# Linear attention and channel mix on one core: q of batch 3 by TensorE, g moved into the x product, and new numbers in the planner

## The chip, the core and the metric

One core of a Trainium2 chip runs the whole kernel. The metric is device microseconds of one execution, the median of several. Times and ratios are of fast runs, except where a slow one is named. A program on one core has no second die to compare with, so "fast" here means within 1.5% of the fastest run of the same kernel. The span of a profile is about 2 us shorter than the time of the same execution (237.8 against 239.78 us before), so spans are compared with spans and times with times.

## The reference, cut to what matters

```python
# 8 batches, 8 heads, 576 positions, head dim 64; d_model 512, d_ff 1024
kv  = einsum('bhsd,bhse->bhde', k, v)
u   = einsum('bhsd,bhde->bhse', q, kv)
x   = u / sqrt(mean(u*u, -1) + 1e-6) * g_norm       # then heads side by side: (8, 576, 512)
x_prev = x shifted by one position
xk, xr = mu_k*x + (1-mu_k)*x_prev, mu_r*x + (1-mu_r)*x_prev
out = sigmoid(xr @ w_r) * (relu(xk @ w_k)**2 @ w_v)
```

The attention of a batch ends in xk and xr. The mix works on nine groups of 512 positions; group g needs the batches that its positions lie in (group 1 needs batches 0 and 1).

## The kernel before

The kernel is written as small pieces of work. A planner inside it (a greedy list scheduler in Python) walks through the pieces with estimated lengths, picks an engine for each, and so fixes the order of the instructions of every engine. The chip then runs each engine's list in that order. A wrong estimate costs nothing by itself, but an instruction that the plan puts too early holds up everything behind it on its engine.

```python
class Planner:
    SHUN = {"DVE": 0.5}          # a penalty when VectorE is one of the choices
    ...
    def run(self, warm=None):
        ...
            ways.append((t + us + self.SHUN.get(eng, 0.0), t, eng))   # earliest end wins
        ...                                                           # (cut)
            if p.land:                                # a piece that starts a DMA
                came = p.end + 1.2
                if p.eng == "POOL":
                    dma = max(dma, came) + p.land
                    p.end = dma + 0.8                 # when the data is believed there
                else:
                    p.end = max(came + p.land, min(dma, came + 2 * p.land)) + 0.8
                    dma = max(dma, came) + p.land
```

Loads of k, v and q are issued by GpSimd (POOL in the profile), one after the other; each has two buffers, so the load of batch b+2 waits until batch b's buffer has been read. q has to be transposed. Batches 0 to 2 do it on TensorE, six 96x128 blocks for each of four head pairs, with a copy out of PSUM (the memory that TensorE writes its products to). Batches 3 to 7 do it by one DMA transpose on the SP queue:

```python
if b >= 3:
    def q_dma(_):
        nc.sync.dma_start_transpose(out=get(qT)..., in_=qin.t...)
    m = add(f"qT dma {b}", {"SP": 3.2}, q_dma, bufs=[qin, qT], due=due(30),
            deps=[loaded[("q", b, 0)]], land=2.5)
else:
    ...                                               # 24 transposes, 4 copies
```

The norm is spread back over 64 columns per head by a product with a matrix selg (0 or g), and x is u times the result, read from PSUM:

```python
nc.vector.tensor_tensor(out=selg[:, tl], in0=rows..., in1=g_all..., op=ALU.mult)     # x4
...
nc.vector.tensor_mul(out=xT.t[:, hs, xs], in0=get(uT)[...], in1=ps.t[:, 0:step, 0:HS])
```

When the plan leaves TensorE idle before the first mix product, it fills the gap with products of zeros ("fillers", one per 0.23 us of the planned gap), which are meant to keep TensorE's clock up. Until 80 us of the plan it also fills some later gaps, before a product that opens a new buffer in PSUM.

Of the kernel before, what the change touches and what calls it, by code (L numbers as in the profile page):

```python
# [36 lines left out]
class Planner:  # L37
    LAT = {"PE": 0.25, "ACT": 0.15, "DVE": 0.12, "POOL": 0.15, "SP": 0.0}

    SWITCH = {"PE": 0.11, "ACT": 1.28}  # L40
    SHUN = {"DVE": 0.5}
    SLACK = {"PE": 0.0}
    STAY = {"PE": 4.0, "ACT": 4.0}

# [33 lines left out]
    def run(self, warm=None):  # L78


        free, order, dma, modes = {}, [], 0.0, {"PE": None, "ACT": None}
        while self.left:
            best = {}
            for p in self.left:
                if any(d.end is None for d in p.deps):
                    continue
                room = self.room(p.bufs)
                if room is None:
                    continue
                ways = []  # L90
                for eng, us in p.on.items():
                    slack = self.SLACK.get(eng, 0.0)
                    t = max(free.get(eng, 0.0), room + slack)
                    for d in p.deps:
                        t = max(t, d.end + (self.LAT[d.eng] + slack if d.eng != eng or d.land else 0.0))
                    ways.append((t + us + self.SHUN.get(eng, 0.0), t, eng))
                _, t, eng = min(ways)
                stay = self.STAY.get(eng, 0.0) if p.mode == modes.get(eng) else 0.0
                best.setdefault(eng, []).append((t, p.due - stay, p))
            picks = []  # L100
            for eng, c in best.items():
                t0 = min(x[0] for x in c)
                picks.append(min((x for x in c if x[0] <= t0 + 0.02), key=lambda x: x[1]) + (eng,))
            t, _, p, p.eng = min(picks, key=lambda x: x[0])
            if warm and p.eng == "PE":
                since, first, until, idle = warm
                gap = t - max(free.get("PE", 0.0), since)
                if first is not None:
                    n, buf = int(gap / 0.23), None
                else:  # L110
                    n, buf = int((gap - 0.3) / 0.23), p.bufs[0] if p.fresh and not p.bufs[0].placed else None
                    n = n if buf is not None and t < until else 0
                if n > 0:
                    order.append(lambda n=n, buf=buf: idle(n, buf))
                if p is first:
                    warm = (since, None, until, idle)
            p.start, p.end = t, t + p.on[p.eng]
            if p.eng in self.SWITCH and p.mode is not None or p.eng == "PE":
                p.end += self.SWITCH[p.eng] * (p.mode != modes[p.eng])
                modes[p.eng] = p.mode  # L120
            free[p.eng] = p.end
            if p.land:

                came = p.end + 1.2
                if p.eng == "POOL":
                    dma = max(dma, came) + p.land
                    p.end = dma + 0.8
                else:
                    p.end = max(came + p.land, min(dma, came + 2 * p.land)) + 0.8
                    dma = max(dma, came) + p.land  # L130
            for b in p.bufs:
                if not b.placed:
                    b.placed = True
                    self.rings[b.tag][self.slots(b.tag)[0][1]] = b
            self.left.remove(p)
            order.append(p)
        for p in order:
            if isinstance(p, Piece):
                p.fn(p.eng)
            else:  # L140
                p()
        return [p for p in order if isinstance(p, Piece)]
# [3 lines left out]
def kernel(  # L146
# [13 lines left out]
    nc = tc.nc  # L160
# [69 lines left out]
    ident8 = const.tile([8, 8], FP32, name="ident8")  # L230
    mu_raw = const.tile([2 * NHP, 128], FP32, name="mu_raw")
    mu_sb = const.tile([128, 2 * NHP], FP32, name="mu_sb")
    g_all = const.tile([128, HD], FP32, name="g_all")
    eps = const.tile([128, 1], FP32, name="eps")
    zeros = const.tile([128, 512], BF16, name="zeros")
    sel = const.tile([128, NHP, 32], BF16, name="sel")
    selg = const.tile([128, NHP, NHP, 2, HD], BF16, name="selg")
    w_r_sb = const.tile([128, NHP, C], BF16, name="w_r")
    w_k_sb = const.tile([128, NHP, F], BF16, name="w_k")
    w_v_sb = const.tile([128, NFC, C], BF16, name="w_v")  # L240
# [4 lines left out]
    def consts_small(_):  # L245
        nc.vector.memset(zeros, 0.0)
        nc.vector.memset(eps, 1e-6)
        ln_table()
        nc.sync.dma_start(out=mu_raw[0:NHP], in_=moe_mu_k.rearrange("(j p) -> j p", p=128))
        nc.sync.dma_start(out=mu_raw[NHP:2 * NHP], in_=moe_mu_r.rearrange("(j p) -> j p", p=128))  # L250
        nc.sync.dma_start(out=g_all, in_=g_norm.rearrange("(o d) -> o d", o=1).broadcast_to([128, HD]))

        nc.vector.memset(sel, 0.0)
        for e in range(2):
            for s in range(NHP):
                nc.vector.memset(sel[64 * e:64 * e + 64, s, 2 * s + e:2 * s + e + 1], 1.0)
# [12 lines left out]
    def consts_selg(_):  # L269

        for tl in range(NHP):
            rows = ident[:, 32 * tl:32 * tl + 2 * NHP].rearrange("p (s e) -> p s e", e=2)
            nc.vector.tensor_tensor(out=selg[:, tl], in0=rows.unsqueeze(3).broadcast_to([128, NHP, 2, HD]),
                                    in1=g_all.unsqueeze(1).unsqueeze(1).broadcast_to([128, NHP, 2, HD]), op=ALU.mult)

    def load_w(dst, src):
        nc.gpsimd.dma_start(out=dst, in_=src.rearrange("(c p) n -> p c n", p=128))
# [8 lines left out]
    def load(b, n, h0, h1, due):  # L286
# [7 lines left out]
        for h in range(h0, h1):  # L294
            loaded[(n, b, h)] = p

    PARTS0 = ((0, 2), (2, 1), (3, 1))
    p_ident = None
    for hp0, n in PARTS0:
# [2 lines left out]
        if p_ident is None:  # L302
            p_ident = add("ident", {"POOL": 0.8}, consts_idents, due=-900 + 0.5)
    p_mu = add("mu", {"DVE": 0.5}, consts_mu, deps=[p_ident], bufs=[p_mu_ps], due=-800)
    p_selg = add("selg", {"DVE": 2.8}, consts_selg, deps=[p_ident], due=-800)
    p_wr = add("load w_r", {"POOL": 0.8}, lambda _: load_w(w_r_sb, moe_w_r), due=-700, land=2.6)
    p_wk = add("load w_k", {"POOL": 0.8}, lambda _: load_w(w_k_sb, moe_w_k), due=-699, land=5.2)
    for n in ("k", "v", "q"):
# [23 lines left out]
    def attention_part(b, part, bufs, ps_buf):  # L332
# [5 lines left out]
        ln, rs = Buf("ln"), Buf("rs")  # L338

        def due(x):  # L340
            return 20 * b - 2 * x if b else -100 - x

        def flat(hp):
            return get(uT)[:, hp].rearrange("q i jj p -> q (i jj p)")
# [14 lines left out]
        def kv_copy(eng, e):  # L359
            for half in range(2):  # L360
# [2 lines left out]

        mm = add(f"kv {b}", {"PE": 0.25 * n}, kv_mm, mode=1, bufs=[pkv, kin, vin, kv], due=due(26),
                 deps=[loaded[(m, b, h)] for m in ("k", "v") for h in (2 * hp0, 2 * (hp0 + n) - 1)] + ([last_rr[0]] if b == 1 else []))
        kvs = [add(f"kv copy {b}", {"DVE": 0.25 + 0.14 * n, "ACT": 0.38 + 0.11 * n}, lambda eng, e=e: kv_copy(eng, e), deps=[mm],
                   bufs=[kv, pkv], due=due(24)) for e in range(2)]


        qts = {}  # L370
        if b >= 3:
            def q_dma(_):
                nc.sync.dma_start_transpose(out=get(qT).rearrange("q h x -> q (h x)").rearrange(
                    "q (y p) -> q y p", p=NP), in_=qin.t.rearrange("p h x -> p (h x)"))

            m = add(f"qT dma {b}", {"SP": 3.2}, q_dma, bufs=[qin, qT], due=due(30), deps=[loaded[("q", b, 0)]], land=2.5)
            qts = {hp: m for hp in hps}
        else:
            for hp in hps:
# [7 lines left out]
                def q_cp(eng, hp, ps):  # L387
                    copy(eng, get(qT)[:, 2 * hp:2 * hp + 2, :], ps.t[:, :, 0:NI * NP])
# [1 line left out]
                ps = ps_buf()  # L390
                m = add(f"qT {b}", {"PE": 0.35}, lambda _, hp=hp, ps=ps: q_tr(_, hp, ps), bufs=[ps, qin, qT], due=due(27),
                        deps=[p_ident, loaded[("q", b, 2 * hp)], loaded[("q", b, 2 * hp + 1)]] + ([last_rr[0]] if b == 1 else []))
                qts[hp] = add(f"qT copy {b}", {"ACT": 0.65, "DVE": 0.75}, lambda eng, hp=hp, ps=ps: q_cp(eng, hp, ps), deps=[m],
                              bufs=[ps, qT], due=due(25))


# [1 line left out]
        for hp in hps:  # L398
# [12 lines left out]
            def u_sq(eng, hp):  # L411
# [3 lines left out]
            ps = ps_buf()  # L415
            m = add(f"u {b}", {"PE": 0.14}, lambda _, hp=hp, ps=ps: u_mm(_, hp, ps), mode=1, deps=kvs + [qts[hp]],
                    bufs=[ps, kv, qT, uT, sq], due=due(22))
            us[hp] = add(f"u copy {b}", {"ACT": 0.69, "DVE": 0.75}, lambda eng, hp=hp, ps=ps: u_cp(eng, hp, ps), deps=[m],
                         bufs=[ps, uT], due=due(21))
            sqs.append(add(f"u sq {b}", {"DVE": 0.46}, lambda eng, hp=hp: u_sq(eng, hp), deps=[us[hp]], bufs=[uT, sq],  # L420
                           due=due(20)))
# [17 lines left out]
            nc.scalar.activation(out=get(rs), in_=ln.t, func=AF.Exp, scale=-0.5)  # L439

        m = add(f"st {b}", {"PE": 0.3}, st_mm, mode=2, deps=sqs, bufs=[pst, sq, ln, rs], due=due(18))
        st = add(f"rs {b}", {"ACT": 0.7}, st_ln, deps=[m], bufs=[pst, ln, rs], due=due(17), mode="ln")


        xms = []
# [1 line left out]
        for hp1 in range(hp0, hp0 + n, step):  # L447
            for half in range(2):
# [11 lines left out]
                def x_mul(_, hp1, cs, xs, ps):  # L460
                    if xT.t is None:
                        nc.vector.memset(get(xT)[:, :, 0:1], 0.0)
                    hs = slice(hp1, hp1 + step)
                    nc.vector.tensor_mul(out=xT.t[:, hs, xs],  # L464
                                         in0=get(uT)[:, hs].rearrange("q h i jj p -> q h (i jj p)")[:, :, cs],
                                         in1=ps.t[:, 0:step, 0:HS])

                ps = ps_buf()
                m = add(f"rr {b}", {"PE": 0.13 * step}, lambda _, hp1=hp1, half=half, ps=ps: rr_mm(_, hp1, half, ps),
# [10 lines left out]
            e.tensor_copy(out=x[:, hsl, 1:NP], in_=x[:, hsl, S:S + NP - 1])  # L480
            e.tensor_tensor(out=get(d)[:, hsl], in0=x[:, hsl, NP:NP + S], in1=x[:, hsl, 0:S], op=ALU.subtract)  # L481

        df = add(f"d {b}", {"DVE": 0.4 * n}, diff, deps=xms, bufs=[xT, d], due=due(11))

        c0 = S * (b % 4)
        order = (("r", xr, NHP), ("k", xk, 0)) if b == 0 else (("k", xk, 0), ("r", xr, NHP))
        for pos, (key, dst, m) in enumerate(order):
# [10 lines left out]
            def blend(_, dst, t):  # L498
# [1 line left out]
                                        op=ALU.add)  # L500

            late = due(10 - 4 * pos) + (50 * pos if b == 0 else 0)
            sc = add(f"t{key} {b}", {"DVE": 0.365 * n, "ACT": 0.7 * n}, lambda eng, m=m, t=t: scale(eng, m, t), deps=[df, p_mu], bufs=[d, t], due=late)
            x_ready[b][key].append(add(f"x{key} {b}", {"DVE": 0.06 + 0.34 * n}, lambda _, dst=dst, t=t: blend(_, dst, t), deps=[sc],
                                       bufs=[xT, t], due=late))

    attention(0, PARTS0)
# [137 lines left out]
```

## Time and profile before

| | before |
|---|---|
| time, median of 3 (lowest to highest); a fourth run came with the result | 239.77 us (239.6 to 240.05) |
| span of the profiled run | 237.8 us |
| TensorE busy | 90% |
| first R product starts | 28.63 us |
| last group (group 8) starts | 214.01 us |

Lines of the page: the span, the busy line, then for TensorE, its granted clock (PEclk, as a share of full speed) and the DMA engines 40 slices of the span (one digit per 5.9 us, in tenths), then the chain of waits by engine and line.

```profile
span 237.8 us, 4055 instructions
...
PE 214.1 (90%) x1669; PEld 103.7 (44%) x1669; DVE 140.7 (59%) x245; ACT 129.5 (54%) x178; POOL 25.1 (11%) x39
...
PE   2989999998583999999898999899899999999981
...
PEclk9999999999887699999999999999999999999997
DMA  3999999999999999999850060024006015015033
...
PE 76%; DMA 8%; DVE 7%; ACT 4%; issue 2%; POOL 1%; DVEq 0%; POOLq 0%
```

PE falls to 5 and 3 tenths in slices 11 and 13 and to no less than 8 anywhere else between head and tail, and PEclk falls to 6 to 8 tenths in slices 11 to 14 (59 to 83 us). The DMA row is at 9 from the second slice to the nineteenth: the loads run without a break until about 110 us. The chain names "DMA qT<-q" for 8% of the span.

In the lines of the mix, L540 is K (xk times w_k), L563 R and L583 V; L354 is kv, L384 a transpose of q, L404 u, L433 the sum of squares, L456 the spreading product, L612 a filler. The stretch from 53.3 to 84.1 us ("the hole" below) in the view of windows (length, then busy time and count of each engine, granted clock, DMA share, GB/s):

```profile
core 0: us, PE busy (x) PEld busy (x) DVE busy (x) ACT busy (x) POOL busy (x), PEclk, DMA share, GB/s
...
53.30:84.10 30.80, 22.45 (x218) 10.10 (x217) 20.89 (x39) 16.34 (x26) 4.62 (x6) 0.83 1.27 195
```

And TensorE's own timeline in it (start and length in us, line, operation, count; in brackets the idle time before it and what ended it):

```profile
57.80 1.89 PE L540 MATMUL mm<-xk,w_k 128*128 128x512 bf16 x8
...
63.25 1.14 PE L354 MATMUL at<-v,k 96*64 96x64 bf16 x48 [2.06 <-DMA v<-in_v_dram]
...
64.77 3.10 PE L540 MATMUL mm<-xk,w_k 128*128 128x512 bf16 x8
...
75.31 0.45 PE L404 MATMUL at<-qT,kv 64*64 64x288 bf16 x4 [4.96 <-DMA qT<-q]
75.69 1.89 PE L540 MATMUL mm<-xk,w_k 128*128 128x512 bf16 x4
...
88.23 1.03 PE L540 MATMUL mm<-xk,w_k 128*128 128x512 bf16 x4
```

Besides 160 small products of attention, this is K and R of group 1; its xk was ready at 57.6 us. They come in parcels between pieces of batches 3 and 4, and each parcel waits for the piece ahead of it: kv of batch 4 for its v (2.06 us), u of batch 3 for the transposed q (4.96 us). After the waits the clock is down: four K products take 1.89 us at 75.69, and 1.03 us at 88.23, when it is up again. TensorE is idle for 8.4 of the 30.8 us (30.80 less 22.45 busy) and runs fillers for 2.8; the rest of what is lost, some 4 us, goes mostly to the slow clock. The wait view (us in total, times, longest) and the SP queue show the transpose and what it blocks:

```profile
POOL q L288 <- DMA qT<-q: 31.9, 2, 16.8
...
PE at L404 <- DMA qT<-q: 5.0, 1, 5.0
...
PE at L354 <- DMA v<-in_v_dram: 2.1, 1, 2.1
```

```profile
55.37 19.71 SPq L373 DMA_TRANSPOSE qT<-q  x2
```

Two transposes are merged in this line, batch 3's among them; it was issued at 55.4 us and landed at 75.3 (19.9 us, the longest by the view of the tile qT). The next load of q may not overwrite the buffer before that, and stands at the head of POOL's list: 16.8 us of the 31.9 us in the first line of the waits.

The head (fillers, the first kv product, the first R product) and the start of the last group.

```profile
4.79 6.21 PE L612 MATMUL mm<-zeros 128*128 128x512 bf16 x18
10.93 0.57 PE L354 MATMUL mm<-v,k 96*64 96x64 bf16 x24
...
28.63 1.89 PE L563 MATMUL mm<-w_r,xr 128*128 128x512 bf16 x8
...
214.01 7.07 PE L540 MATMUL mm<-xk,w_k 128*128 128x512 bf16 x32
```

### The profile page before, as it was taken

The page shows a single profiled execution, that of the slowest core. Times are in us where ns is not written, and L with a number is a line of the kernel's source. Part 1 is how long each engine was busy: PE and PEld are TensorE (multiplying, and loading weights), DVE is VectorE, ACT ScalarE, POOL GpSimd, SP SyncE. Part 2 cuts the span into 40 slices and gives each one's busy share as a digit, 9 for nine tenths or more (in the row PEclk, how much of TensorE's full clock was granted, in tenths as well). Part 3 has the DMA queues.
Part 4 walks back from the last instruction along what each step waited for, and adds up shares of the span by engine and source line. Part 5 has one row for each costly group of instructions (what it writes and reads, how often), then busy time and mean ns, then how long its engine had stood idle before and what let it go on. Part 6 is the DMA issues. An engine that isn't in the chain of part 4 may idle for free.

```text
span 237.8 us, 4055 instructions
## 1 busy us (share of the span) xinstructions
PE 214.1 (90%) x1669; PEld 103.7 (44%) x1669; DVE 140.7 (59%) x245; ACT 129.5 (54%) x178; POOL 25.1 (11%) x39
## 2 busy tenths in 40 slices
PE   2989999998583999999898999899899999999981
PEld 1443454554330355345434466444444444444430
DVE  1436938379487369977973895697487324224222
ACT  2075697828531691994789557666954513604500
POOL 8553021212001320010000000000000000000000
PEclk9999999999887699999999999999999999999997
DMA  3999999999999999999850060024006015015033
GB/s 41 197 207 207 204 207 203 204 204 241 188 160 176 209 202 158 195 256 100 197 123 0 4 176 3 0 61 119 0 0 164 12 26 156 0 28 152 0 88 88
DMA packets 38627, 29.46 MB, mean 124 GB/s; under 512 B 13513, under 2 KB 33489, under 8 KB 38609
## 3 DMA queue, kind: packets, MB, share of 16 engines
q0 software_dynamic: 21008, 16.78, 47.0%
q1 hardware_dynamic: 17600, 12.43, 24.7%
q8 instruction: 13, 0.21, 0.4%
q14 instruction: 6, 0.04, 0.1%
HBM read 33.59 MB, written 9.44 MB: 181 GB/s over the span
## 4 chain that ended last, share of the span: by engine, by line
PE 76%; DMA 8%; DVE 7%; ACT 4%; issue 2%; POOL 1%; DVEq 0%; POOLq 0%
PE mm L540 25%; PE mm L583 24%; PE mm L563 13%; DMA qT<-q 8%; PE mm L612 5%; PE at L404 3%; PE at L456 2%; DVE out L587 2%; DVE xT L464 2%; ACT sig L568 1%; PE at L384 1%; DVE d L481 1%; PE at L433 1%; ACT kv L216 1%; ACT uT L216 1%
## 5 line engine op out<-in xcount | busy, mean ns | idle before, releaser
L540 PE MATMUL mm<-xk,w_k 128*128 128x512 bf16 (+1 forms) x320 | 70.1, 369 | 1.3 <-DVE out L587 1.3
L583 PE MATMUL mm<-w_v,sqk 128*128 128x512 bf16 x288 | 66.2, 379 | 1.9 <-DVE out L587 1.7
L544 ACT ACTIVATE relu<-mm 128x1024 bf16<-128x1024 f32 x36 | 36.8, 1023 | 38.8 <-PE mm L540 37.4
L540 PEld LDWEIGHTS <-w_k 128*128 128x128 bf16 x320 | 30.2, 100 | 31.9 <-issue 5.9
L583 PEld LDWEIGHTS <-sqk 128*128 128x128 bf16 x288 | 27.6, 98 | 32.3 <-issue 2.8
L587 DVE TENSOR_TENSOR out<-mm,sig 128x1024 f32<-128x1024 f32 (+1 forms) x20 | 22.3, 1116 | 27.3 <-PE mm L583 27.2
L547 DVE TENSOR_TENSOR sqk<-relu 128x1024 bf16<-128x1024 bf16 x36 | 24.7, 690 | 19.6 <-ACT relu L544 19.6
L563 PE MATMUL mm<-w_r,xr 128*128 128x512 bf16 x144 | 33.2, 381 | 0.0
L464 DVE TENSOR_TENSOR xT<-uT,at 128x576 bf16<-128x576 bf16 (+1 forms) x31 | 21.8, 732 | 14.0 <-PE at L456 14.0
L496 ACT ACTIVATE t<-d,mu_sb 128x576 bf16<-128x576 bf16 x30 | 21.0, 768 | 16.0 <-DVE d L481 14.6
L216 ACT CAST uT<-at 128x576 bf16<-128x576 f32 x24 | 14.5, 640 | 18.5 <-PE at L404 18.5
L563 PEld LDWEIGHTS <-xr 128*128 128x128 bf16 x144 | 13.7, 98 | 16.7 <-issue 0.7
L568 ACT ACTIVATE sig<-mm 128x1024 bf16<-128x1024 f32 x18 | 18.1, 1023 | 4.3 <-PE mm L563 4.2
L612 PE MATMUL mm<-zeros 128*128 128x512 bf16 x69 | 20.0, 418 | 0.0
L413 DVE TENSOR_TENSOR sq<-uT 128x576 bf16<-128x576 bf16 x32 | 13.9, 455 | 8.1 <-ACT uT L216 7.7
L456 PE MATMUL at<-rs,selg 128*128 128x144 bf16 x120 | 11.8, 229 | 1.8 <-DVE xT L464 1.8
L456 PEld LDWEIGHTS <-selg 128*128 128x128 bf16 x128 | 9.7, 99 | 7.7 <-issue 3.2
L404 PE MATMUL at<-qT,kv 64*64 64x288 bf16 x116 | 8.4, 321 | 5.0 <-DMA qT<-q 5.0
L288 POOL DMA_DIRECT2D q<-in_q_dram x10 | 7.3, 734 | 40.1 <-DMA qT<-q 31.9
L499 DVE TENSOR_TENSOR xk<-t,xT 128x2304 bf16<-128x2304 bf16 (+2 forms) x10 | 11.1, 1114 | 0.5 <-ACT t L496 0.4
L481 DVE TENSOR_TENSOR d<-xT 128x2304 bf16<-128x2304 bf16 (+2 forms) x10 | 11.2, 1118 | 0.3
L288 POOL DMA_DIRECT2D k<-in_k_dram x10 | 7.5, 752 | 35.7 <-PE at L354 32.0
(51 smaller groups left out, 136.7 us busy)
## 6 DMA issues: line engine op xcount, KB each, us to landing
out_dram<-out SPq DMA_DIRECT2D x24, 192.0 KB, 2.5
k<-in_k_dram POOLq DMA_DIRECT2D x7, 576.0 KB, 14.9
v<-in_v_dram POOLq DMA_DIRECT2D x7, 576.0 KB, 18.1
q<-in_q_dram POOLq DMA_DIRECT2D x7, 576.0 KB, 18.0
out_dram<-out SPq DMA_DIRECT2D x24, 128.0 KB, 2.4
out_dram<-out SPq DMA_DIRECT2D x24, 64.0 KB, 2.1
w_k<-in_moe_w_k_dram POOLq DMA_DIRECT2D x1, 1024.0 KB, 11.7
w_v<-in_moe_w_v_dram POOLq DMA_DIRECT2D x1, 1024.0 KB, 22.4
```

The lines of the kernel that those rows point to most:

```text
L216: nc.scalar.copy(out=dst, in_=src)
L456: nc.tensor.matmul(get(ps)[:, i, SEC * c:SEC * c + SEC], selg[:, tl, sub].rearrange("p e d -> p (e d)"), rs.t, start=True, stop=True)
L464: nc.vector.tensor_mul(out=xT.t[:, hs, xs], in0=get(uT)[:, hs].rearrange("q h i jj p -> q h (i jj p)")[:, :, cs], in1=ps.t[:, 0:step, 0:HS])
L496: nc.scalar.mul(out=dst, in_=d.t[:, hp, :], mul=by)
L540: nc.tensor.matmul(get(ps)[:, fc % 2, a0:a1], w_k_sb[:, cc, 128 * fc:128 * fc + 128], xk[:, cc, x0:x0 + a1 - a0], start=(cc == 0), stop=(c ...
L544: nc.scalar.activation(out=get(rt), in_=ps.t, func=AF.Relu)
L547: nc.vector.tensor_mul(out=get(sqk)[:, 2 * f2:2 * f2 + 2, :], in0=rt.t, in1=rt.t)
L563: nc.tensor.matmul(get(ps)[:, ci % 2, :], xr[:, cc, n0:n0 + 128], w_r_sb[:, cc, :], start=(cc == 0), stop=(cc == NHP - 1))
L568: nc.scalar.activation(out=get(sg), in_=ps.t, func=AF.Sigmoid)
L583: nc.tensor.matmul(get(ps)[:, ci % 2, :], sqk.t[:, fc, 128 * ci:128 * ci + 128], w_v_sb[:, fc, :], start=(fc == 0), stop=(fc == NFC - 1))
L587: nc.vector.tensor_mul(out=get(ot)[:, xs, :], in0=ps.t[:, xs, :], in1=sg.t[:, xs, :])
L612: nc.tensor.matmul(get(buf or warm)[:, 0, :], zeros[:, 0:128], zeros, start=True, stop=True)
```

## The change

The intent: keep VectorE's work small (selg becomes a 0/1 matrix that ScalarE copies; g enters the x product as a per-partition scalar), take one more batch of q away from the DMA queues, and tell the planner how long things really take. "due" in the code is the planner's priority: of the pieces that can start equally early on an engine, the one with the smallest due goes first.

```diff
-    SHUN = {"DVE": 0.5}
+    SHUN = {"DVE": 0.1}
...
+                    if eng == "POOL" and p.land and len(queue) >= 8:
+                        t = max(t, queue[-8])
...
-                came = p.end + 1.2
+                came = max(p.end + 1.2, 3.5)
...
-                    p.end = dma + 0.8
+                    p.end = dma + 1.5
+                    queue.append(p.end)
...
-                    p.end = max(came + p.land, min(dma, came + 2 * p.land)) + 0.8
+                    p.end = max(came + p.land, min(dma, came + 2 * p.land)) + 1.5
...
-            nc.vector.tensor_tensor(out=selg[:, tl], in0=rows..., in1=g_all..., op=ALU.mult)
+            nc.scalar.copy(out=selg[:, tl], in_=rows...)
...
-    p_selg = add("selg", {"DVE": 2.8}, consts_selg, ...)
+    p_selg = add("selg", {"ACT": 2.4}, consts_selg, ...)
...
-            return 20 * b - 2 * x if b else -100 - x          # due of attention pieces
+            return 20 * b - 2 * x - 4 if b else -100 - x
...
-        if b >= 3:
+        if b >= DMA_T:                                        # DMA_T = 4
...
-            m = add(f"qT dma {b}", {"SP": 3.2}, ..., land=2.5)
+            m = add(f"qT dma {b}", {"SP": 7.8}, ..., land=3.5)
...
-                    nc.vector.tensor_mul(out=xT..., in0=uT..., in1=ps...)
+                    nc.vector.scalar_tensor_tensor(out=xT..., in0=uT..., scalar=g_col,
+                        in1=ps..., op0=ALU.mult, op1=ALU.mult)
```

Cut: g_col is loaded by two small DMAs in place of the broadcast g_all; the planner starts with ScalarE's ln table loaded; the lengths of seven kinds of piece were refitted (for example the copy of qT on VectorE from 0.75 to 0.46 us).

More of the change, by code (lines that the diff above doesn't have):

```diff
@@ L78, in run @@
     def run(self, warm=None):
-        free, order, dma, modes = {}, [], 0.0, {"PE": None, "ACT": None}
+        free, order, queue, dma, modes = {}, [], [], 0.0, {"PE": None, "ACT": "ln"}
         while self.left:
@@ L232 @@
     mu_sb = const.tile([128, 2 * NHP], FP32, name="mu_sb")
-    g_all = const.tile([128, HD], FP32, name="g_all")
     eps = const.tile([128, 1], FP32, name="eps")
@@ L237 @@
     selg = const.tile([128, NHP, NHP, 2, HD], BF16, name="selg")
+    g_col = const.tile([128, 1], FP32, name="g_col")
     w_r_sb = const.tile([128, NHP, C], BF16, name="w_r")
@@ L250, in consts_small @@
         nc.sync.dma_start(out=mu_raw[NHP:2 * NHP], in_=moe_mu_r.rearrange("(j p) -> j p", p=128))
-        nc.sync.dma_start(out=g_all, in_=g_norm.rearrange("(o d) -> o d", o=1).broadcast_to([128, HD]))
+        for e in range(2):
+            nc.sync.dma_start(out=g_col[HD * e:HD * e + HD], in_=g_norm.rearrange("(d o) -> d o", o=1))
         nc.vector.memset(sel, 0.0)
@@ L272, in consts_selg @@
             rows = ident[:, 32 * tl:32 * tl + 2 * NHP].rearrange("p (s e) -> p s e", e=2)
-            nc.vector.tensor_tensor(out=selg[:, tl], in0=rows.unsqueeze(3).broadcast_to([128, NHP, 2, HD]),
-                                    in1=g_all.unsqueeze(1).unsqueeze(1).broadcast_to([128, NHP, 2, HD]), op=ALU.mult)
+            nc.scalar.copy(out=selg[:, tl], in_=rows.unsqueeze(3).broadcast_to([128, NHP, 2, HD]))
     def load_w(dst, src):
@@ L295, in load @@
             loaded[(n, b, h)] = p
+    DMA_T = 4
     PARTS0 = ((0, 2), (2, 1), (3, 1))
@@ L304 @@
     p_mu = add("mu", {"DVE": 0.5}, consts_mu, deps=[p_ident], bufs=[p_mu_ps], due=-800)
-    p_selg = add("selg", {"DVE": 2.8}, consts_selg, deps=[p_ident], due=-800)
+    p_selg = add("selg", {"ACT": 2.4}, consts_selg, deps=[p_ident], due=-800)
     p_wr = add("load w_r", {"POOL": 0.8}, lambda _: load_w(w_r_sb, moe_w_r), due=-700, land=2.6)
@@ L365, in attention_part @@
                  deps=[loaded[(m, b, h)] for m in ("k", "v") for h in (2 * hp0, 2 * (hp0 + n) - 1)] + ([last_rr[0]] if b == 1 else []))
-        kvs = [add(f"kv copy {b}", {"DVE": 0.25 + 0.14 * n, "ACT": 0.38 + 0.11 * n}, lambda eng, e=e: kv_copy(eng, e), deps=[mm],
+        kvs = [add(f"kv copy {b}", {"DVE": 0.34 + 0.13 * n, "ACT": 0.32 + 0.105 * n}, lambda eng, e=e: kv_copy(eng, e), deps=[mm],
                    bufs=[kv, pkv], due=due(24)) for e in range(2)]
         qts = {}
-        if b >= 3:
+        if b >= DMA_T:
             def q_dma(_):
@@ L374, in q_dma @@
                     "q (y p) -> q y p", p=NP), in_=qin.t.rearrange("p h x -> p (h x)"))
-            m = add(f"qT dma {b}", {"SP": 3.2}, q_dma, bufs=[qin, qT], due=due(30), deps=[loaded[("q", b, 0)]], land=2.5)
+            m = add(f"qT dma {b}", {"SP": 7.8}, q_dma, bufs=[qin, qT], due=due(30), deps=[loaded[("q", b, 0)]], land=3.5)
             qts = {hp: m for hp in hps}
@@ L392, in attention_part @@
                         deps=[p_ident, loaded[("q", b, 2 * hp)], loaded[("q", b, 2 * hp + 1)]] + ([last_rr[0]] if b == 1 else []))
-                qts[hp] = add(f"qT copy {b}", {"ACT": 0.65, "DVE": 0.75}, lambda eng, hp=hp, ps=ps: q_cp(eng, hp, ps), deps=[m],
+                qts[hp] = add(f"qT copy {b}", {"ACT": 0.64, "DVE": 0.46}, lambda eng, hp=hp, ps=ps: q_cp(eng, hp, ps), deps=[m],
                               bufs=[ps, qT], due=due(25))
@@ L417, in attention_part @@
                     bufs=[ps, kv, qT, uT, sq], due=due(22))
-            us[hp] = add(f"u copy {b}", {"ACT": 0.69, "DVE": 0.75}, lambda eng, hp=hp, ps=ps: u_cp(eng, hp, ps), deps=[m],
+            us[hp] = add(f"u copy {b}", {"ACT": 0.64, "DVE": 0.76}, lambda eng, hp=hp, ps=ps: u_cp(eng, hp, ps), deps=[m],
                          bufs=[ps, uT], due=due(21))
@@ L441, in attention_part @@
         m = add(f"st {b}", {"PE": 0.3}, st_mm, mode=2, deps=sqs, bufs=[pst, sq, ln, rs], due=due(18))
-        st = add(f"rs {b}", {"ACT": 0.7}, st_ln, deps=[m], bufs=[pst, ln, rs], due=due(17), mode="ln")
+        st = add(f"rs {b}", {"ACT": 0.74}, st_ln, deps=[m], bufs=[pst, ln, rs], due=due(17), mode="ln")
         xms = []
@@ L463, in x_mul @@
                     hs = slice(hp1, hp1 + step)
-                    nc.vector.tensor_mul(out=xT.t[:, hs, xs],
-                                         in0=get(uT)[:, hs].rearrange("q h i jj p -> q h (i jj p)")[:, :, cs],
-                                         in1=ps.t[:, 0:step, 0:HS])
+                    nc.vector.scalar_tensor_tensor(
+                        out=xT.t[:, hs, xs], in0=get(uT)[:, hs].rearrange("q h i jj p -> q h (i jj p)")[:, :, cs],
+                        scalar=g_col, in1=ps.t[:, 0:step, 0:HS], op0=ALU.mult, op1=ALU.mult)
                 ps = ps_buf()
@@ L481, in diff @@
             e.tensor_tensor(out=get(d)[:, hsl], in0=x[:, hsl, NP:NP + S], in1=x[:, hsl, 0:S], op=ALU.subtract)
-        df = add(f"d {b}", {"DVE": 0.4 * n}, diff, deps=xms, bufs=[xT, d], due=due(11))
+        df = add(f"d {b}", {"DVE": 0.34 + 0.33 * n}, diff, deps=xms, bufs=[xT, d], due=due(11))
         c0 = S * (b % 4)
@@ L502, in attention_part @@
             late = due(10 - 4 * pos) + (50 * pos if b == 0 else 0)
-            sc = add(f"t{key} {b}", {"DVE": 0.365 * n, "ACT": 0.7 * n}, lambda eng, m=m, t=t: scale(eng, m, t), deps=[df, p_mu], bufs=[d, t], due=late)
-            x_ready[b][key].append(add(f"x{key} {b}", {"DVE": 0.06 + 0.34 * n}, lambda _, dst=dst, t=t: blend(_, dst, t), deps=[sc],
+            sc = add(f"t{key} {b}", {"DVE": 0.06 + 0.29 * n, "ACT": 0.08 + 0.68 * n}, lambda eng, m=m, t=t: scale(eng, m, t), deps=[df, p_mu], bufs=[d, t], due=late)
+            x_ready[b][key].append(add(f"x{key} {b}", {"DVE": 0.15 + 0.3 * n}, lambda _, dst=dst, t=t: blend(_, dst, t), deps=[sc],
                                        bufs=[xT, t], due=late))
```

## The prediction

> **What bounds the kernel now.** TensorE, with one hole. PE is busy 90% of a 237.8 us span (page) and 76% of the chain of waits. The timeline of PE splits the span:
>
> - 0 to 28.8 us, head: a latency chain of batch 0 (first k, v land at 10.9 us). Its end is VectorE, nearly without a gap from 21.7 to 28.8.
> - To 53.3: PE nearly dense.
> - 53.3 to 84.1, the hole. Useful there: 48 K/R matmuls at 0.216 us (10.4), 32 of u (2.0), 96 of kv (1.8), 16 of st (0.4), 16 of rr (1.0): 15.5 of 30.8 us, about 15 us lost. Named waits: kv of batch 4 for its v load (2.1 us), and u of batch 3 for the DMA transpose of q (5.0 us; issue to landing 19.9). The lulls cost more: in 75.3 to 84.1 the granted clock averaged 0.68 and K/R matmuls stood 0.43-0.47 us apart instead of 0.216. That agrees with the Trainium skill, "TensorE: Matmul & The Clock Gate", Part 1 (half clock after an idle window, 427 against 216 ns at N=512).
> - 84.1 to 179.6: dense but for waits of 0.6 to 1.3 us; a stage takes 20.4 to 21 us, VectorE about 75% busy.
> - Then pure PE plus a tail.
>
> The hole is an ordering error, not missing work: K, R and V of group 1 need batches 0 and 1 alone, but stand in PE's queue behind pieces of batches 3 and 4 that the planner believed ready. It allows a DMA transpose 3.2 us issue and 2.5 transfer; the trace shows 7.8 median issue, 15.2 to landing, while loads fill the queues (DMA 0.9 or more until about 110 us). The q load behind it held POOL 16.8 us.
>
> **What the change does.**
> 1. Batch 3's q goes to TensorE: 24 transposes, 4 x 0.26 = +1.04 us of PE, and four copies (0.64 ACT or 0.46 DVE). Removed: the 19.9 us transpose and the block of POOL. This closes most of the hole.
> 2. The planner's landings, queue depth and op lengths now resemble the trace.
> 3. Attention is due earlier by 4, bringing xk of batch 1 (57.6 us now) forward.
> 4. selg leaves VectorE (4 x 0.686 us, 6.6 to 9.1) for ScalarE (estimate 4 x 0.58 from its 0.64 for 576 columns). Both idle then: about 0.
> 5. g enters the x product as a per-partition scalar. It reads the same f32 PSUM operand (0.753 us for 576, about one element per cycle already), so 0.75 again, x34: 0.
> 6. The smaller penalty on DVE moves some copies from ACT to DVE: 0 to 1 us either way.
>
> **Sum.** 237.8 - 15 (hole) + 1.0 (transposes) + about 1.5 of small new waits = 225 span; the measured time stands 2 us above the span, so 227; reordering elsewhere gives about 1.5. Predicted 225.5 us, 220.5 to 233. Estimated floor: 28.8 + 181 of dense PE + 4.4 tail = 214 span, 216 timed.
>
> Chances: faster by over 2% 0.93, within 2% 0.05, slower 0.02.
>
> **What would show it.** One DMA transpose fewer (4); granted clock 1.0 throughout 53 to 84 us; PE idle behind the qT transpose and v loads below 2 us; first R still at 27.5 to 30 us; x multiplications 0.73 to 0.80 us; stages after 120 us still 20 to 21 us; start of the last group (214.0) near 202.
>
> **What would make it wrong.** Transposes of batch 4 colliding with loads and opening a second hole near 80 to 95 us; a slower x product lengthening VectorE's run at the head; a reordered head moving the first R by over 2 us.

## The result, and the profile after

| | before | after |
|---|---|---|
| time, median (lowest to highest) | 239.87 us (239.6 to 240.05, 4 runs) | 227.17 us (226.73 to 227.84, 4 runs) |
| ratio, 95% interval | | 0.9474 (0.9447 to 0.9500) |
| span of the profiled run | 237.8 us | 224.8 us |
| first R product starts | 28.63 us | 30.34 us |
| last group starts | 214.01 us | 201.07 us |

A ratio is the mean time of one kernel's fast runs over the mean of the other's fast runs of the same rounds; it is not quite the ratio of the medians in the table.

The page after:

```profile
span 224.8 us, 4075 instructions
...
PE 207.6 (92%) x1668; PEld 104.2 (46%) x1694; DVE 144.8 (64%) x253; ACT 124.0 (55%) x172; POOL 25.7 (11%) x39
...
PE   2997999999789989999999999999999999999971
...
PEclk9999999999999999999999999999999999999999
DMA  4999999999999999999960240024033033024033
...
PE 86%; DVE 6%; ACT 3%; issue 2%; POOL 1%; DVEq 0%; POOLq 0%
```

PEclk is 9 in every slice and the chain no longer names the DMA transpose. The same piece of the program (from u of batch 2 to the end of R of group 1) now lasts from 54.8 to 75.6 us, where it lasted from 53.3 to 84.1 (columns as above):

```profile
54.80:75.60 20.80, 17.93 (x231) 9.50 (x235) 19.62 (x34) 16.29 (x26) 2.30 (x3) 1.00 1.31 197
```

```profile
59.69 1.89 PE L544 MATMUL mm<-xk,w_k 128*128 128x512 bf16 x8 [0.99 <-DVE xk L503]
...
67.04 1.03 PE L544 MATMUL mm<-xk,w_k 128*128 128x512 bf16 x4
...
71.44 0.32 PE L408 MATMUL at<-qT,kv 64*64 64x288 bf16 x4
...
201.07 7.07 PE L544 MATMUL mm<-xk,w_k 128*128 128x512 bf16 x31
```

K and R are still cut into parcels by pieces of attention, but the pieces are ready when their turn comes. The wait for xk of batch 1 (0.99 us) is the longest in the stretch. The view of waits has no line any more in which a product of TensorE waits for a load or a transpose; a load of q is still blocked by a transpose for 16.0 us, once instead of twice, from 78.7 to 94.8 us, when k, v and q of batch 6 are already under way:

```profile
POOL q L291 <- DMA qT<-q: 16.0, 1, 16.0
```

Two things moved that I had predicted to stay. The head is later, behind a longer run of fillers:

```profile
4.77 8.13 PE L616 MATMUL mm<-zeros 128*128 128x512 bf16 x28
12.84 0.57 PE L358 MATMUL mm<-v,k 96*64 96x64 bf16 x24
...
30.34 1.89 PE L567 MATMUL mm<-w_r,xr 128*128 128x512 bf16 x8
```

One execution tells the length of the head only roughly: the same 28 fillers took from 8.13 to 9.18 us in the profiles of the six kernels that have them, and 18 took from 5.44 to 6.31 us in another six.

And the x product, in the groups by shape (busy time and the mean of one in ns, then the idle time before them), before and after:

```profile
L464 DVE TENSOR_TENSOR xT<-uT,at 128x576 bf16<-128x576 bf16 x29 | 20.9, 751 | 14.0 <-PE at L456 14.0
...
L464 DVE TENSOR_TENSOR xT<-uT,at 128x288 bf16<-128x288 bf16 x2 | 0.9, 449 | 0.0
```

```profile
L468 DVE SCALAR_TENSOR_TENSOR xT<-uT,g_col,at 128x576 bf16<-128x576 bf16 x29 | 22.6, 811 | 2.7 <-PE at L460 2.3
...
L468 DVE SCALAR_TENSOR_TENSOR xT<-uT,g_col,at 128x288 bf16<-128x288 bf16 x2 | 0.9, 509 | 0.0
```

It costs 60 ns more for 576 columns and 60 ns more for 288: at these two widths a price per instruction, not per column.

Where the 13.0 us of span came from, by cutting both timelines of TensorE at the same pieces of the program:

| stretch, ending with | before | after | difference |
|---|---|---|---|
| start to first R | 28.63 | 30.34 | +1.7 |
| to u of batch 2 | 53.3 - 28.6 = 24.7 | 54.8 - 30.3 = 24.5 | -0.2 |
| to the end of R of group 1 | 84.1 - 53.3 = 30.8 | 75.6 - 54.8 = 20.8 | -10.0 |
| to the start of the last group | 214.0 - 84.1 = 129.9 | 201.1 - 75.6 = 125.5 | -4.4 |
| to the end | 23.8 | 23.7 | -0.1 |

### The profile page after: what moved, and what is told of

The parts are those of the page before. It is cut to its first block, busy times and chain, and to the rows that moved or that the text cites. A ratio compares the mean times of both kernels' runs of the same rounds, so it can differ in the third digit from the quotient of the medians.

```text
span 224.8 us, 4075 instructions
## 1 busy us (share of the span) xinstructions
PE 207.6 (92%) x1668; PEld 104.2 (46%) x1694; DVE 144.8 (64%) x253; ACT 124.0 (55%) x172; POOL 25.7 (11%) x39
## 4 chain that ended last, share of the span: by engine, by line
PE 86%; DVE 6%; ACT 3%; issue 2%; POOL 1%; DVEq 0%; POOLq 0%
PE mm L544 27%; PE mm L587 27%; PE mm L567 14%; PE mm L616 7%; PE at L460 3%; PE at L408 2%; PE at L358 2%; DVE xT L468 1%; PE at L388 1%; PE at L437 1%; DVE out L591 1%; DVE sq L417 1%; ACT kv L219 1%; DVE d L485 1%; DVE xk L503 1%
## 5 line engine op out<-in xcount | busy, mean ns | idle before, releaser
L587 PE MATMUL mm<-w_v,sqk 128*128 128x512 bf16 x279 | 65.0, 379 | 2.3 <-DVE out L591 1.7
L544 PE MATMUL mm<-xk,w_k 128*128 128x512 bf16 (+1 forms) x313 | 65.7, 358 | 1.4 <-DVE xk L503 1.0
L544 PEld LDWEIGHTS <-w_k 128*128 128x128 bf16 x320 | 30.3, 98 | 29.6 <-issue 1.7
L551 DVE TENSOR_TENSOR sqk<-relu 128x1024 bf16<-128x1024 bf16 x36 | 24.7, 690 | 24.1 <-ACT relu L548 24.1
L468 DVE SCALAR_TENSOR_TENSOR xT<-uT,g_col,at 128x576 bf16<-128x576 bf16 (+1 forms) x31 | 23.6, 791 | 2.7 <-PE at L460 2.3
L616 PE MATMUL mm<-zeros 128*128 128x512 bf16 x71 | 19.5, 412 | 0.4 <-issue 0.3
L219 ACT CAST uT<-at 128x576 bf16<-128x576 f32 x19 | 11.6, 637 | 9.0 <-PE at L408 8.9
L417 DVE TENSOR_TENSOR sq<-uT 128x576 bf16<-128x576 bf16 x32 | 13.3, 454 | 0.8 <-ACT uT L219 0.7
L460 PE MATMUL at<-rs,selg 128*128 128x144 bf16 x120 | 11.1, 226 | 0.7 <-DVE xT L468 0.7
L616 PEld LDWEIGHTS <-zeros 128*128 128x128 bf16 x76 | 7.3, 104 | 8.2 <-issue 2.5
L503 DVE TENSOR_TENSOR xr<-t,xT 128x2304 bf16<-128x2304 bf16 (+2 forms) x10 | 11.0, 1113 | 0.0
```

The source lines that it names most:

```text
L460: nc.tensor.matmul(get(ps)[:, i, SEC * c:SEC * c + SEC], selg[:, tl, sub].rearrange("p e d -> p (e d)"), rs.t, start=True, stop=True)
L468: nc.vector.scalar_tensor_tensor(out=xT.t[:, hs, xs], in0=get(uT)[:, hs].rearrange("q h i jj p -> q h (i jj p)")[:, :, cs], scalar=g_col, ...
L503: nc.vector.tensor_tensor(out=dst[:, hsl, c0:c0 + S], in0=t.t[:, 0:n, :], in1=xT.t[:, hsl, 0:S], op=ALU.add)
L544: nc.tensor.matmul(get(ps)[:, fc % 2, a0:a1], w_k_sb[:, cc, 128 * fc:128 * fc + 128], xk[:, cc, x0:x0 + a1 - a0], start=(cc == 0), stop=(c ...
L551: nc.vector.tensor_mul(out=get(sqk)[:, 2 * f2:2 * f2 + 2, :], in0=rt.t, in1=rt.t)
L587: nc.tensor.matmul(get(ps)[:, ci % 2, :], sqk.t[:, fc, 128 * ci:128 * ci + 128], w_v_sb[:, fc, :], start=(fc == 0), stop=(fc == NFC - 1))
```

## The experiments

Twelve kernels ran, in three sets. The kernel before ran beside each set at 239.56, 239.67 and 239.64 us (medians), so times of different sets can be laid side by side to a few tenths of a us. Ratios are to the kernel before. All results are correct but one. One point of method: a change of one number in the planner lets it plan anew, so such a kernel can differ from its parent anywhere. Where an experiment keeps the plan, it says so.

| kernel | time, median (runs) | ratio, 95% |
|---|---|---|
| before, batch 3 to TensorE only | 234.64 us (4) | 0.9788 (0.9737 to 0.9839) |
| before, three DMA numbers only | 241.88 us (4) | 1.0089 (1.0041 to 1.0138) |
| before, both of these | 234.34 us (6, one of them slow; 233.95 of the five fast) | 0.9778 (0.9748 to 0.9809) |
| before, batch 3's transpose taken away, order kept (wrong result) | 231.08 us (4) | 0.9638 (0.9589 to 0.9686) |
| before, g in the x product, order kept | 240.27 us (6) | 1.0020 (0.9993 to 1.0047) |
| after | 227.17 us (4) | 0.9474 (0.9447 to 0.9500) |
| after, batch 3 back to the DMA | 235.26 us (4) | 0.9825 (0.9775 to 0.9874) |
| after, the same, planner told it is 6 us later | 234.39 us (6) | 0.9788 (0.9762 to 0.9815) |
| after, old due of attention | 230.96 us (6) | 0.9637 (0.9615 to 0.9659) |
| after, old penalty on VectorE | 239.66 us (6) | 1.0007 (0.9982 to 1.0033) |
| after, g back in selg, order kept | 227.29 us (6) | 0.9478 (0.9452 to 0.9505) |
| after, 18 fillers at the start | 225.67 us (6) | 0.9406 (0.9377 to 0.9435) |
| after, 18 fillers and g back in selg | 225.60 us (6) | 0.9412 (0.9385 to 0.9440) |

### Is it the transpose of batch 3, or the planner's numbers?

My theory was that the hole is made by batch 3's late transpose, that item 1 of the change closes most of it, and that it is an ordering error at bottom. Four kernels.

The kernel before with one number changed:

```diff
-        if b >= 3:
+        if b >= 4:
```

> The kernel before, with q of batch 3 also transposed by TensorE and nothing else changed (the planner keeps its old numbers). Theory T (the DMA transpose of batch 3 is what opens the hole, so moving it is enough): the granted clock is 1.0 through 53 to 84 us and the time is 226 to 230 us. Rival P (the planner's too short numbers are the cause, batch 3 only the first to show it): a hole of about 10 us or more opens again at batch 4, between 70 and 95 us, and the time stays at 234 to 240 us.

Measured: 234.64 us, 4.9 us less than before and inside P's range, at its lower end. The stretch around 60 to 75 us is nearly closed, but a hole opens at 92 to 99 us:

```profile
94.71 1.49 PE L354 MATMUL at<-v,k 96*64 96x64 bf16 x48 [2.56 <-DMA v<-in_v_dram]
```

The product waits for a v that was loaded late, because that load stood behind a load of q, which held POOL for 14.3 us. The profile names no releaser for that; the buffer that the load writes is read by batch 4's transpose, issued at 64.9 us.

```profile
77.68 0.78 POOL L288 DMA_DIRECT2D q<-in_q_dram  x1 [14.33 <-issue]
...
79.21 0.77 POOL L288 DMA_DIRECT2D v<-in_v_dram  x1
```

The v issued at 79.21 landed at 94.7. This is P's prediction in kind (the hole moves to a later batch), smaller in size. By the order of the loads it is batch 6; a later run, below, calls it batch 5.

The reverse, the changed kernel with batch 3 on the DMA again:

```diff
-    DMA_T = 4
+    DMA_T = 3
```

> The changed kernel with batch 3's q again transposed by DMA, but planned with the new numbers. Theory T: the hole comes back, 235 to 240 us. Rival P: the planner puts other work in front of the late transpose; 225 to 231 us, with the granted clock above 0.95 everywhere.

Measured: 235.26 us. T's range held. Telling the planner 7.8 and 3.5 us did not save the plan: TensorE still waits for the transposes of two batches, and the granted clock is at 8 tenths in two slices.

```profile
73.92 0.45 PE L408 MATMUL at<-qT,kv 64*64 64x288 bf16 x4 [3.13 <-DMA qT<-q]
...
86.12 0.32 PE L408 MATMUL at<-qT,kv 64*64 64x288 bf16 x4 [1.71 <-DMA qT<-q]
```

The numbers alone:

```diff
-    {"SP": 3.2} ... land=2.5, and 0.8 us to every landing
+    {"SP": 7.8} ... land=3.5, and 1.5 us to every landing
```

> The kernel before with only three planner numbers changed: the DMA transpose takes 7.8 us to issue and 3.5 to transfer, and every landing comes 0.7 us later. Batch 3 stays on the DMA. Rival P in its strong form: these numbers alone win at least half of the 12.7 us, 226 to 233 us. Theory T: under 3 us, 237 us or more.

Measured: 241.88 us, slower by 0.9%, with TensorE waiting 5.1 us for a transpose.

```profile
73.81 0.70 PE L404 MATMUL at<-qT,kv 64*64 64x288 bf16 x8 [5.08 <-DMA qT<-q]
```

P in its strong form is dead: these three numbers win nothing alone.

The kernel before with its order kept and the transpose gone:

```diff
             def q_dma(_):
+                if b == 3:
+                    nc.vector.memset(get(qT), 0.0)
+                    return
```

> The kernel before, its order on every engine kept, with batch 3's DMA transpose replaced by a memset of the same tile (the result is wrong on purpose). This takes away the wait and the block of POOL without the 1 us of TensorE transposes and without any new plan. If the late transpose is all of the hole, about 13 us go: 226 to 228 us. If the landing of batch 4's v and the late xk of batch 1 hold a large part of it, 5 to 9 us go: 231 to 235 us.

Measured: 231.08 us (the result is wrong, on purpose). That is in the second range. The wait for batch 3's transpose and its block of POOL are worth 8.5 us in the old order; the rest of the 12.7 us does not come from them. Note that this kernel is also spared the 1 us of TensorE transposes.

### If the planner knew, would order alone do?

```diff
-    DMA_T = 4
+    DMA_T = 3
...
+                    if p.name == "qT dma 3":
+                        p.end += 6.0
```

> The changed kernel with batch 3 by DMA, and the planner told 6 us more for that one transpose, which is then about as late in the plan as the trace of the run before showed it (issued at 54.7 us, landed at 73.8). If the hole is an ordering error alone, as the prediction said, the planner puts K, R and V of group 1 in front and the time is 227 to 230 us. If there is too little ready work to put in front (K of group 1 starts only at 59.9 us, and the two PSUM buffers and VectorE limit it), waits remain and it stays at 232 us or more.

Measured: 234.39 us, 0.9 us less than without the knowledge, and not clear of the spread. The planner did what was hoped for batch 3: all of R of group 1 and a quarter of K of group 2 now stand ahead of its u, and TensorE does not wait there. But the hole moved to batch 4, whose transpose stands behind batch 3's on the SP queue:

```profile
87.40 0.32 PE L410 MATMUL at<-qT,kv 64*64 64x288 bf16 x4 [4.39 <-DMA qT<-q]
```

So "an ordering error, not missing work" was too simple. Here a late transpose, put right in the plan, handed the delay on to the transpose behind it. Whether a plan with five DMA transposes and no hole exists was not settled; this one was not it.

The two halves together, on the kernel before:

```diff
-        if b >= 3:
+        if b >= 4:
...
-    {"SP": 3.2} ... land=2.5, and 0.8 us to every landing
+    {"SP": 7.8} ... land=3.5, and 1.5 us to every landing
```

> The kernel before with both halves together: batch 3 on TensorE, and the three planner numbers of the DMA transposes and landings; no other change. Alone they gave -5.1 and +2.1 us. If the second half of the gain is that the planner then also places batches 4 to 7 rightly (the hole at 92 to 99 us, kv of batch 5 waiting 2.56 us for its v, goes away): 227 to 230 us. If it comes from the earlier due of attention, the smaller penalty on VectorE, the queue depth or the op lengths instead: 233 us or more.

Measured: 233.95 us in the five fast runs (the sixth, at 238.16, was slow), 0.7 us below batch 3 alone and within the spread of these runs (233.48 to 235.34). The three DMA numbers are worth nothing clear with it either. The wait for a late v stays:

```profile
95.11 0.95 PE L354 MATMUL at<-v,k 96*64 96x64 bf16 x48 [1.90 <-DMA v<-in_v_dram]
```

What is left of the gain, some 7 us, must come from the other planner changes, since the move of g is worth nothing (below).

### The other planner changes

```diff
-            return 20 * b - 2 * x - 4 if b else -100 - x
+            return 20 * b - 2 * x if b else -100 - x
```

> The changed kernel with the due times of attention as before (not 4 earlier). If the earlier due matters for the waits after 84 us, 1.5 to 4 us slower, with waits of 0.6 us at each stage back; if not, within 0.7 us.

Measured: 230.96 us, 3.8 slower than the changed kernel, and the stage waits of the kernel before are back, one at each stage:

```profile
121.55 0.41 PE L460 MATMUL at<-rs,selg 128*128 128x144 bf16 x4 [0.66 <-DVE xT L468]
...
142.54 0.41 PE L460 MATMUL at<-rs,selg 128*128 128x144 bf16 x4 [0.66 <-DVE xT L468]
```

In the profiled spans (229.3 against 224.8 us), 3.4 of the 4.5 us lie between u of batch 2 and the last group, where those waits are; the other 1.1 us is in the head of that execution, whose first R product starts at 31.39 us (its 28 fillers took 9.18 us, where those of the changed kernel took 8.13).

```diff
-    SHUN = {"DVE": 0.1}
+    SHUN = {"DVE": 0.5}
```

> The changed kernel with the old penalty of 0.5 us on VectorE in the planner's choice of engine. I predicted 0 to 1 us either way for it. If spreading the copies over both engines shortens the chains of attention, it is 1 to 3 us slower.

Measured: 239.66 us. The whole gain is gone with this one number, and I had given it 0 to 1 us either way. The trace does not show slower copies (the copy of u by ScalarE takes 639 ns, 637 in the changed kernel). It shows another order: kv of batch 2 comes at 49.4 us (44.4 in the changed kernel), so its buffer is free later and k of batch 4 is issued at 51.0 us (45.7); then a load of q holds POOL for 18.1 us behind a DMA transpose.

```profile
50.99 0.77 POOL L291 DMA_DIRECT2D k<-in_k_dram  x1 [0.60 <-PE at L358]
...
74.48 0.77 POOL L291 DMA_DIRECT2D q<-in_q_dram  x1 [18.10 <-DMA qT<-q]
```

The hole is between 91 and 107 us, with the same two waits as in the kernel before; the granted clock is at 5 and 7 tenths in slices 17 and 18, after them:

```profile
PEclk9999999979999999579999999999999999999999
...
93.51 1.14 PE L358 MATMUL at<-v,k 96*64 96x64 bf16 x48 [1.96 <-DMA v<-in_v_dram]
...
99.72 0.45 PE L408 MATMUL at<-qT,kv 64*64 64x288 bf16 x4 [4.48 <-DMA qT<-q]
```

From 60 to 120 us TensorE is idle for 8.2 us (1.8 in the changed kernel). A smaller loss lies at 44 to 52 us, where TensorE waits for VectorE's x products of batch 1 and its clock falls to 7 tenths (slice 9).

Whether the choice of engines for the copies has any worth of its own was not separated from the order that the planner drew from it; an experiment with the old engines in the new order did not run.

### g in the x product

Two kernels that keep the plan and the order, and move only g: the changed kernel with the old selg and the plain product, and the kernel before with the new ones.

In the changed kernel (the planner still counts selg as ScalarE's):

```diff
-            nc.scalar.copy(out=selg[:, tl], in_=rows...)
+            nc.vector.tensor_tensor(out=selg[:, tl], in0=rows..., in1=g_all..., op=ALU.mult)
...
-                    nc.vector.scalar_tensor_tensor(out=xT..., in0=uT..., scalar=g_col, in1=ps..., ...)
+                    nc.vector.tensor_mul(out=xT..., in0=uT..., in1=ps...)
```

> The changed kernel, its plan and order kept, with g put back into the spreading matrices (built by VectorE) and the x product a plain product again. The x product of 576 columns should fall from 0.81 to 0.75 us. Theory: VectorE is not the bound after the head, so only the six products on the head's chain count: 0.2 to 0.6 us faster, first R 0.2 to 0.5 us earlier. Rival (VectorE, 90% busy between 50 and 120 us, bounds that stage): 1.5 to 2 us faster, 34 times 0.06.

Measured: 227.29 us against 227.17. Neither the 0.2 to 0.6 us of my theory nor the 1.5 to 2 of the rival shows; the difference is within the spread of the runs.

In the kernel before, the same edit the other way round:

```diff
-            nc.vector.tensor_tensor(out=selg[:, tl], in0=rows..., in1=g_all..., op=ALU.mult)
+            nc.scalar.copy(out=selg[:, tl], in_=rows...)
...
-                    nc.vector.tensor_mul(out=xT..., in0=uT..., in1=ps...)
+                    nc.vector.scalar_tensor_tensor(out=xT..., in0=uT..., scalar=g_col, in1=ps..., ...)
```

> The kernel before, its plan and order kept, with only the first of the named changes: 0/1 spreading matrices built by ScalarE, g in the x product. I predicted about 0 for it. With 0.06 us more for each x product: 0 to 1 us slower, never faster by more than 0.3 us.

Measured: 240.27 us, a ratio of 1.0020 with an interval that holds 1. The 2 us more of VectorE (34 products at 60 ns) cost no time that is clear of the spread, in either kernel. They are not wholly hidden: in this one the three stage waits of TensorE for an x product grow from 0.60 to 0.65 us.

### The head

```diff
+                if len(order) < 40 and n > 18:
+                    n = 18
                 if n > 0:
                     order.append(lambda n=n, buf=buf: idle(n, buf))
```

> The changed kernel with the first run of filler matmuls cut from 28 to 18, the number of the kernel before; nothing else moves. In the changed kernel the fillers end at 12.9 us and the first kv product starts at 12.84 us instead of 10.93, and the first R product at 30.34 instead of 28.63. If the fillers hold the head back: kv at about 10.9 us, first R at 28.5 to 28.9, and 1.5 to 1.9 us less in all. If k and v simply land later in the changed kernel (rival): kv waits for a load, and the time stays within 0.5 us.

Measured: 225.67 us, 1.5 less than the changed kernel.

```profile
4.77 5.67 PE L619 MATMUL mm<-zeros 128*128 128x512 bf16 x18
10.36 0.57 PE L361 MATMUL mm<-v,k 96*64 96x64 bf16 x24
...
43.24 0.95 PE L361 MATMUL at<-v,k 96*64 96x64 bf16 x48 [1.20 <-DMA v<-in_v_dram]
```

In the profiled run kv starts at 10.36 and the first R at 27.86 us, 2.5 us earlier than in the changed kernel. Only 1.3 us of that reach the end of the span: the last line shows kv of batch 2 waiting 1.20 us for its v. The loads did not come earlier with the head, so it runs into them at 43 us. The rival (k and v land later) is dead: kv did not wait for a load.

Both edits, the 18 fillers and the plain x product, in one kernel:

```diff
+                    n = 18
...
+                    nc.vector.tensor_mul(out=xT..., in0=uT..., in1=ps...)
```

> The changed kernel with both: 18 fillers and g in the spreading matrices. If the two effects add, 1.7 to 2.5 us below the changed kernel, so about 225 us.

Measured: 225.60 us, the same as with the fillers alone, so the effects do not add; there was no second effect. The fastest kernel is the changed one with 18 fillers, 225.67 us (225.60 with g back in selg is no different).

## Why the prediction was right, and where it was not

The time was right: 225.5 predicted, 227.17 measured, inside the range of 220.5 to 233. Its parts were less so; that the sum came out so near was partly luck, as the sum below shows.

1. The hole (53.3 to 84.1 us) was the place of the gain. Predicted net of the TensorE transposes and small new waits: -12.5 us; measured -10.0. The useful work there is 16.5 us with the transposes (15.5 + 1.04) and the stretch takes 20.8, so 4.3 us are still lost where I allowed 1.5 (TensorE is idle for 2.9 of them, 20.80 less 17.93 busy).
2. "Reordering elsewhere gives about 1.5" was mis-sized: -4.4 us. The earlier due of attention is a good part of it: without it, the span from u of batch 2 to the last group is 3.4 us longer.
3. The head was predicted unmoved ("first R still at 27.5 to 30 us"). It moved by +1.7, to 30.34. The prediction took the head for a wait for loads ("first k, v land at 10.9 us"). By the trace they had landed at 8.1 and 9.5 us (issued at 1.3 and 2.1, landed 6.8 and 7.4 us later), and kv started at 10.93, when the fillers ended: the fillers held it up in the kernel before too. The step I did not think of: later landings in the plan mean a longer planned gap, and the planner fills it with real products that hold up the first kv. Cutting them to 18 gave back 1.5 us of time. The three DMA numbers account for 3 of the 10 new fillers (21 in that kernel, with the first R unmoved at 28.60). By the code the others fit the new floor of 3.5 us under the first transfer, planned for 2.0 us before (1.5 us later, six or seven fillers); no run tested it alone.
4. "Batch 3's q goes to TensorE ... This closes most of the hole" held only together with the other planner changes: alone it gives 5 us of 12.7. Without it the changed kernel loses 8 us. The two do not add.
5. "The planner's landings, queue depth and op lengths now resemble the trace" was taken for a cause. The three DMA numbers alone give +2.1 us, and nothing clear on top of batch 3. The queue depth, the op lengths, the floor of 3.5 us and the start with the ln table were not tried alone.
6. "0 to 1 us either way" for the penalty on VectorE was the largest error: going back to 0.5 costs 12.5 us. By the trace this goes through the order of loads and transposes, not through the length of copies; no experiment separated the two.
7. "bringing xk of batch 1 (57.6 us now) forward" did not happen: it was ready at 59.6 us, 2.0 later than before, 1.7 of which is the later head. The earlier due pays in the later stages.
8. g and selg: about 0 predicted, about 0 measured. The x product was to stay at 0.73 to 0.80 us and is 0.81.
9. Confirmed marks: four DMA transposes; the granted clock at full through the former hole; no wait of TensorE behind the qT transpose or a v load; the last group at 201.07 against "near 202"; stages after 120 us still 20.7 us (u of batch 6 starts at 119.4, u of batch 7 at 140.0).

Points 1 to 3 in a sum: 237.8 - 10.0 - 4.4 + 1.7 - 0.3 = 224.8. My -12.5 - 1.5 + 0 came to nearly the same because the errors cancelled (the hole gave 2.5 less, the later stages 2.9 more, the head took 1.7), and that was luck.

The Trainium skill was used in two places. "TensorE: Matmul & The Clock Gate", Part 1, says that the clock halves after an idle window and that N=512 products then follow each other at 427 ns in place of 216. The trace agrees: after the wait for q the granted clock was 0.50 from 75.3 to 79.7 us and K products within a run of four started up to 427 ns apart (the prediction had 0.43 to 0.47 us), against 216 ns when warm, so the waits cost more than their length. "DMA: Bandwidth & Descriptors", Issuing engines are not separate DMA queues, says that DMAs issued from different engines run on the same 16 DMA engines and interleave. The trace agrees with it: in the kernel before, the transposes on the SP queue took 15.2 us (median) to land beside the loads from POOL, and 6.5 us at the least, when the loads were done.

## What to carry to other kernels

In a kernel that is planned by estimates, look for the wait that takes the clock down and for the queue that a blocked item holds shut; the loads behind a blocked load were part of the cost here, one or two batches later (with batch 3 alone on TensorE, and with the old penalty). Do not price a scheduler's constant by the operation that it is named after: price it by the order that it produces, and test each constant alone and each one undone, since here three constants alone were worth +2 us, one change alone -5, and undoing another cost 12.5, where the whole was -12.7. Work that fills a gap (fillers) belongs to the critical path as soon as the gap is shorter than planned.

## What the Trainium skill lacked or had wrong

- "DMA: Bandwidth & Descriptors", Latency and other measured facts, gives 261 GB/s for a DMA transpose, measured on one kernel. Here one transpose of 0.59 MB (96 x 3072 elements of two bytes) took, from issue to landing, 6.5 us at the least in the kernel before and 4.4 us at the least in any run (the changed kernel with the old due, and with the old penalty): about 90 and 134 GB/s over issue and transfer together. In the kernel before it took 15.2 us in the median and 19.9 at most beside the loads. The page's figure may leave out the issue, so it is not shown to be wrong. The page has no figure for a transpose beside other traffic, nor that its issue stretches too: 3.07 us alone and up to 8.4 us beside the loads.
- "VectorE: DVE Perf Modes", Scalar operands, names no price for a per-partition scalar. The x product with one costs 60 ns more than the plain product, at 288 and at 576 columns alike (449 to 509, 751 to 811 ns).
